# Units of four heads, spread MoE work and elementwise steps on GpSimd in a fused attention and MoE kernel

## The chip, the cores and the metric

The kernel runs on one core of a Trainium2 chip. Times are microseconds of device time of one launch; a kernel's time is the median of its runs. The profile describes one of these runs, taken with the hardware profiler; its "span" is the time from the first to the last instruction, and in the profiled run of the changed kernel the time is 1.8 us above the span. PE is the matrix engine, DVE the vector engine, ACT the scalar engine, POOL the GpSimd engine and SP the engine that only issues transfers here. "L230" is line 230 of the kernel in question; "MoE" is the program's name for the two dense products with an ELU between them.

## The reference

Eight batches of eight heads of 576 rows of 64 values go through an attention with exponential features. Their results, put side by side, are the 4608 rows of 512 values of the dense part.

```python
def phi(x):                                   # x: batch, head, 576, 64
    proj = np.einsum('bhsd,df->bhsf', x, w_phi)                    # 128 features
    proj = proj - np.max(np.abs(proj), axis=-1, keepdims=True)
    return np.concatenate([np.exp(proj), np.exp(-proj)], axis=-1)
q_p, k_p = phi(q), phi(k)
kv  = np.einsum('bhsf,bhsd->bhfd', k_p, v)
z   = np.sum(k_p, axis=2)
num = np.einsum('bhsf,bhfd->bhsd', q_p, kv)
den = np.einsum('bhsf,bhf->bhs', q_p, z)[..., None] + 1e-06
x   = (num / den)                             # as 4608 rows of 512
h   = x @ w_in                                # 512 -> 2048
g   = np.where(h > 0, h, np.exp(np.minimum(h, 0)) - 1)             # ELU
out = g @ w_out                               # 2048 -> 512
```

With m the largest |projection| of a row, the two halves of a row's features are exp(p) exp(-m) and exp(-p) exp(m). For a query row the factor exp(-m) falls out of num / den (but for the 1e-06), while the two halves keep different weights, 1 and exp(2m). The kernel before leaves that weight out. The changed kernel puts it back ("query maximum restored"), which is added work.

## The kernel before

One unit of attention is a pair of heads. Key maxima `m_k`, key exponentials `EK` and the factors `em` are made first; `em` scales the values into `vs`, on DVE, in many small pieces:

```python
for g0, gcnt in s_groups:                     # 3 groups of up to 2 row tiles
    ...                                       # pk: projection of the keys, in PSUM
    nc.vector.tensor_reduce(m_k[...], pk_v, axis=AX.X, op=ALU.max, apply_absolute_value=True)
    nc.scalar.activation(EK[..., 0, :], pk_v, ACT.Exp, scale=1.0)
    nc.scalar.activation(EK[..., 1, :], pk_v, ACT.Exp, scale=-1.0)
    nc.scalar.activation(em[:, 0, ...], m_k[...], ACT.Exp, scale=-1.0)
    nc.scalar.activation(em[:, 1, ...], m_k[...], ACT.Exp, scale=1.0)
    for hi in range(2):
        for sg in range(2):
            nc.vector.tensor_tensor(vs[hi][:, sg, ...], v_aug[hi][...], em[...], op=ALU.mult)
```

Then come the query exponentials `Eq`, the products `pkv` (keys by values) and `pn` (queries by `pkv`), and the division into `x_pair`, which five transposes turn for the dense part. The query maximum exists behind a switch that is off:

```python
EXACT_QMAX = False
...
if EXACT_QMAX:
    ...                                       # second projection, m_q, w_s = exp(2 m_q)
    nc.vector.tensor_tensor(tot, pnum[1], w_s[...], op=ALU.mult)
    nc.vector.tensor_tensor(tot, tot, pnum[0], op=ALU.add)
else:
    ...                                       # both halves summed in PSUM by PE
nc.vector.tensor_scalar_add(den, num_src[:, :, D], 1e-6)
nc.vector.reciprocal(rec, den)
nc.vector.tensor_tensor(x_pair[...], num_src[:, :, 0:D], rec..., op=ALU.mult)
```

In a unit of the first GEMM, the ELU takes three instructions: the exponential on ACT, and two on DVE.

```python
nc.scalar.activation(e_sb, ph, ACT.Exp)
nc.vector.tensor_scalar(u_sb, e_sb, 1.0, 1.0, op0=ALU.min, op1=ALU.subtract)
nc.vector.tensor_tensor(gT[:, jt], u_sb, ph, op=ALU.max)
```

All weights are loaded before the first q and k, on POOL's queue. A chunk of 512 rows becomes MoE work once its batches are done, and it is laid into the pairs by a quota of at least one GEMM unit per pair; what is left follows at the end.

The softmax here doesn't subtract the row's maximum and nothing guards it: scores larger than these inputs give would overflow.

## Time and profile before

| what | kernel before | where it is from |
|---|---|---|
| time | 530.67 us (527.86 to 531.39), 3 runs | timed runs |
| span, mean granted clock | 524.4 us, 0.948 | profiled run |
| busy: PE, DVE, ACT, POOL | 78%, 69%, 61%, 49% | totals of the page |
| first matmul | 26.9 us | order of time |
| two pairs of heads in the middle | 22.7 us (2 x 11.35; 27 pairs end by 334 us, the first at 39 us) | order of time |
| last two MoE chunks | 461 to 521 us | order of time |

A busy share is an average over the start, the middle and the end. Each has another limit here: transfers in the first 27 us, the serial chain of a pair up to 334 us, PE itself after that. The prediction below shows the lines in question.

### The profile page before, as it was taken

The page shows a single profiled execution, that of the slowest core. Times are in us where ns is not written, and L with a number is a line of the kernel's source. Part 1 is how long each engine was busy: PE and PEld are TensorE (multiplying, and loading weights), DVE is VectorE, ACT ScalarE, POOL GpSimd, SP SyncE. Part 2 cuts the span into 40 slices and gives each one's busy share as a digit, 9 for nine tenths or more (in the row PEclk, how much of TensorE's full clock was granted, in tenths as well). Part 3 has the DMA queues.
Part 4 walks back from the last instruction along what each step waited for, and adds up shares of the span by engine and source line. Part 5 has one row for each costly group of instructions (what it writes and reads, how often), then busy time and mean ns, then how long its engine had stood idle before and what let it go on. Part 6 is the DMA issues. An engine that isn't in the chain of part 4 may idle for free.

```text
span 524.4 us, 9742 instructions
## 1 busy us (share of the span) xinstructions
PE 408.5 (78%) x3200; PEld 222.5 (42%) x3200; DVE 364.1 (69%) x1358; ACT 319.5 (61%) x904; POOL 258.3 (49%) x400
## 2 busy tenths in 40 slices
PE   0056667678976679977789778977997999989997
PEld 0034444345543345534455444443544454434433
DVE  2055568989788988798986789479459579174470
ACT  0046568777568876787866788479257367153441
POOL 6299999967677767776676666460000000000000
PEclk9997668979989989998999899999999999989999
DMA  8989988955866756877567655660110100200102
GB/s 157 185 53 59 58 57 55 58 40 38 106 61 40 46 37 62 100 46 46 36 56 85 58 35 34 90 59 2 42 40 2 56 25 1 81 1 31 51 0 80
DMA packets 124817, 28.45 MB, mean 54 GB/s; under 512 B 117600, under 2 KB 119648, under 8 KB 124768
## 3 DMA queue, kind: packets, MB, share of 16 engines
q0 software_dynamic: 119584, 18.41, 47.7%
q1 hardware_dynamic: 5184, 9.44, 4.9%
q8 instruction: 25, 0.41, 0.3%
q14 instruction: 24, 0.20, 0.1%
HBM read 36.77 MB, written 9.44 MB: 88 GB/s over the span
## 4 chain that ended last, share of the span: by engine, by line
PE 49%; DVE 21%; ACT 21%; DMA 4%; issue 3%; POOL 1%; POOLq 0%; DVEq 0%; ACTq 0%
PE po L127 21%; PE ph L102 13%; DVE vs L243 5%; ACT EK L230 4%; ACT EK L227 4%; PE pk L212 4%; DVE gT L116 4%; DVE u_sb L112 4%; ACT Eq L266 4%; DVE x_pair L353 3%; DMA w_out_sb<-in_moe_w_out_dram 3%; PE pn L341 3%; PE tr L198 3%; ACT Eq L268 2%; PE xt L369 2%
## 5 line engine op out<-in xcount | busy, mean ns | idle before, releaser
L102 PE MATMUL ph<-xT_sb,w_in_sb 128*128 128x512 bf16 x576 | 158.9, 396 | 19.3 <-DVE gT L116 15.7
L127 PE MATMUL po<-w_out_sb,gT 128*128 128x512 bf16 x576 | 133.4, 379 | 0.3 <-DVE gT L116 0.2
L110 ACT ACTIVATE e_sb<-ph 128x512 f32<-128x512 f32 x144 | 85.2, 640 | 39.5 <-PE ph L102 39.1
L116 DVE TENSOR_TENSOR gT<-u_sb,ph 128x512 bf16<-128x512 bf16 x144 | 97.2, 681 | 1.8
L112 DVE TENSOR_SCALAR u_sb<-e_sb 128x512 bf16<-128x512 f32 x144 | 62.3, 442 | 42.4 <-ACT e_sb L110 41.8
L102 PEld LDWEIGHTS <-w_in_sb 128*128 128x128 bf16 x576 | 55.4, 101 | 75.8 <-issue 39.3
L243 DVE TENSOR_TENSOR vs<-v_aug,em 128x130 bf16<-128x130 bf16 (+1 forms) x384 | 75.6, 265 | 9.6 <-ACT em L233 9.1
L127 PEld LDWEIGHTS <-gT 128*128 128x128 bf16 x576 | 54.3, 98 | 59.6 <-issue 3.6
L168 POOL DMA_DIRECT2D q_pair<-in_q_dram x64 | 55.2, 866 | 43.4 <-PE tr L198 37.8
L266 ACT ACTIVATE Eq<-pq 128x288 bf16<-128x288 f32 x128 | 59.1, 462 | 24.6 <-PE pq L259 24.3
L220 DVE TENSOR_REDUCE m_k<-pk 128x4 f32<-128x512 f32 (+1 forms) x96 | 52.1, 594 | 14.3 <-PE pk L212 14.2
L268 ACT ACTIVATE Eq<-pq 128x288 bf16<-128x288 f32 x128 | 60.9, 476 | 0.0
L168 POOL DMA_DIRECT2D k_pair<-in_k_dram x64 | 57.1, 898 | 5.1 <-DMA w_out_sb<-in_moe_w_out_dram 4.4
L184 POOL DMA_DIRECT2D v_aug<-in_v_dram x64 | 53.7, 863 | 10.0 <-DVE den L351 5.2
L227 ACT ACTIVATE EK<-pk 128x512 bf16<-128x512 f32 (+1 forms) x96 | 52.5, 547 | 4.5 <-DVE m_k L220 4.5
L188 POOL DMA_DIRECT2D v_aug<-in_v_dram x64 | 40.8, 639 | 27.8 <-DVE vs L243 27.8
L276 PEld LDWEIGHTS <-EK 128*128 128x128 bf16 x640 | 32.4, 102 | 51.2 <-issue 20.1
L135 ACT COPY o_sb<-po 128x512 f32<-128x512 f32 x27 | 15.8, 586 | 62.0 <-PE po L127 62.0
L230 ACT ACTIVATE EK<-pk 128x512 bf16<-128x512 f32 (+1 forms) x96 | 53.5, 558 | 0.0
L259 PE MATMUL pq<-qTp,w_phi_both 128*128 128x288 bf16 x128 | 32.6, 300 | 19.9 <-ACT EK L230 18.6
L276 PE MATMUL pkv<-vs,EK 128*128 128x65 bf16 x640 | 36.1, 201 | 14.4 <-ACT EK L230 8.0
L174 POOL DMA_DIRECT2D k_pair<-in_k_dram x64 | 43.9, 685 | 4.5 <-DMA w_out_sb<-in_moe_w_out_dram 4.5
(46 smaller groups left out, 458.4 us busy)
## 6 DMA issues: line engine op xcount, KB each, us to landing
out_dram<-o_sb SPq DMA_DIRECT2D x36, 256.0 KB, 2.0
q_pair<-in_q_dram POOLq DMA_DIRECT2D x64, 64.0 KB, 2.6
k_pair<-in_k_dram POOLq DMA_DIRECT2D x64, 64.0 KB, 2.7
v_aug<-in_v_dram POOLq DMA_DIRECT2D x64, 64.0 KB, 2.8
w_in_sb<-in_moe_w_in_dram POOLq DMA_DIRECT2D x4, 512.0 KB, 7.1
w_out_sb<-in_moe_w_out_dram POOLq DMA_DIRECT2D x4, 512.0 KB, 15.9
q_pair<-in_q_dram POOLq DMA_DIRECT2D x64, 8.0 KB, 2.1
k_pair<-in_k_dram POOLq DMA_DIRECT2D x64, 8.0 KB, 2.3
```

The lines of the kernel that those rows point to most:

```text
L102: nc.tensor.matmul(ph[:, 0:csz], w_in_sb[:, ct, jt * P:(jt + 1) * P], xT_sb[:, ct, t0:t0 + csz], start=(ct == 0), stop=(ct == N_CT - 1),)
L110: nc.scalar.activation(e_sb[:, 0:csz], ph[:, 0:csz], ACT.Exp)
L112: nc.vector.tensor_scalar(u_sb[:, 0:csz], e_sb[:, 0:csz], 1.0, 1.0, op0=ALU.min, op1=ALU.subtract,)
L116: nc.vector.tensor_tensor(gT[:, jt, 0:csz], u_sb[:, 0:csz], ph[:, 0:csz], op=ALU.max)
L127: nc.tensor.matmul(po[0:tsz], gT[:, jt, tt * P:tt * P + tsz], w_out_sb[:, jt, :], start=(jt == 0), stop=(jt == N_JT - 1),)
L168: nc.gpsimd.dma_start(out=dst[:, 0:full_st, hi * D:(hi + 1) * D], in_=src[b, h, 0:full_st * P, :].rearrange("(t p) d -> p t d", p=P),)
L227: nc.scalar.activation(EK[:, g0:g0 + gcnt, :, 0, :], pk_v, ACT.Exp, scale=1.0)
L230: nc.scalar.activation(EK[:, g0:g0 + gcnt, :, 1, :], pk_v, ACT.Exp, scale=-1.0)
L243: nc.vector.tensor_tensor(vs[hi][:, sg, g0:g0 + gcnt], v_aug[hi][:, g0:g0 + gcnt], em[:, sg, g0:g0 + gcnt, hi:hi + 1].to_broadcast((P, gcn ...
L266: nc.scalar.activation(eq[:, 0, c0:c0 + half_S], pq, ACT.Exp, scale=1.0)
L268: nc.scalar.activation(eq[:, 1, c0:c0 + half_S], pq, ACT.Exp, scale=-1.0)
L276: nc.tensor.matmul(pkv[:, hi, sg, :], EK[:, ti, hi, sg, :], vs[hi][:, sg, ti, :], start=(ti == 0), stop=(ti == n_st - 1),)
```

## The change

The intent: fewer and larger instructions, DVE relieved, PE fed evenly. A unit of attention is four heads. The 64 tail rows of the heads are packed together. A chunk of 512 rows per batch is MoE work, spread over the two units of the next batch, step by step; the eight tails of 64 rows make the ninth chunk. q and k of the first unit are loaded ahead of the weights. The ELU's subtract, the scaling `vs` (and its tail `vst`) and the division `x` (and `xt`) go to POOL. The query maximum is back. The core of the diff:

```diff
 # 1. loads: q/k first, weights between the units' loads, v on SP's queue
-    for ct in range(N_CT):
-        nc.gpsimd.dma_start(out=w_in_sb[:, ct, :], in_=w_in_r[:, ct, :])
-    ...
+    load_quad(0)
+    load_tails(0, 4)
+    load_quad(1)
+    load_w_in()
+    load_quad(2)
+    load_w_out()
+    load_tails(4, NQ)
 # 2. vs: four heads' values, one instruction per head, on POOL
-                    nc.vector.tensor_tensor(
-                        vs[hi][:, sg, g0:g0 + gcnt],
-                        ...
+            for hh in range(4):
+                nc.gpsimd.tensor_tensor(
+                    vs[:, hh],
+                    vb[:, hh:hh + 1].to_broadcast((P, 2, NT, D1)),
+                    em[:, :, 4 * hh:4 * hh + 4, None].to_broadcast((P, 2, NT, D1)),
+                    op=ALU.mult,
+                )
+            ...                                   # vst: two more for the tails
 # 3. query maximum: a second projection per head, and a weighted sum on DVE
+        def q_head(hh):
+            project(st["qT"], hh, st["m_q"])
+            ...
+            nc.scalar.activation(w, st["m_q"], ACT.Exp, scale=2.0)
+            ...
+            nc.vector.tensor_tensor(tot, pn[1], st["w"][...], op=ALU.mult)
+            nc.vector.tensor_tensor(tot, tot, pn[0], op=ALU.add)
 # 4. division, on POOL
-            nc.vector.tensor_tensor(
-                x_pair[:, :, hi * D:(hi + 1) * D], ...
+                nc.gpsimd.tensor_tensor(
+                    st["x"][:, s, :, c, :],
+                    st["tot"][:, hh, :, 0:D],
+                    rec[:, 4 * hh:4 * hh + 4, None].to_broadcast((P, NT, D)),
+                    op=ALU.mult,
+                )
+            ...                                   # xt: one more for the tails
 # 5. ELU: subtract on POOL, minimum and maximum in one instruction on DVE
-        nc.vector.tensor_scalar(
-            u_sb[:, 0:csz], e_sb[:, 0:csz], 1.0, 1.0, op0=ALU.min, op1=ALU.subtract,
-        )
-        nc.vector.tensor_tensor(gT[:, jt, 0:csz], u_sb[:, 0:csz], ph[:, 0:csz], op=ALU.max)
+        nc.gpsimd.tensor_scalar(u_sb, e_sb, -1.0, 1.0, op0=ALU.add, op1=ALU.mult)
+        nc.vector.scalar_tensor_tensor(
+            gTs[ch][:, jt, :], u_sb, 0.0, ph, op0=ALU.min, op1=ALU.max
+        )
 # 6. MoE spread over the steps of the units
-                quota = max(1, len(pending_moe) // remaining_pairs)
+        share = len(pending) if qd == 1 else len(pending) // 2
+        for n, step in enumerate(steps):
+            step()
+            upto = share * (n + 1) // len(steps)
+            while done < upto:
+                pending.pop(0)()
+                done += 1
```

The steps of a unit are, in this order: transposes, five key projections, `k_scale` (makes em, vs, vst), five query projections, the query features, two `kv`, four heads of output, the tail, `divide`, and the transposes of x.

## The prediction

> **What bounds the kernel now.** I read the totals first, then the slices, then the start, then one head pair in order of time, then the end.
>
> ```profile
> span 524.4 us, 9742 instructions
> PE 408.5 (78%) x3200; PEld 222.5 (42%) x3200; DVE 364.1 (69%) x1358; ACT 319.5 (61%) x904; POOL 258.3 (49%) x400
> ...
> PE   0056667678976679977789778977997999989997
> ...
> DMA  8989988955866756877567655660110100200102
> ```
>
> No engine is full. PE is idle for 524.4 - 408.5 = 116 us: all of the first two slices (13.1 us each), some 30% of the long middle, little at the end. The order of time says why:
>
> ```profile
> 14.66 0.54 POOL L174 DMA_DIRECT2D q_pair<-in_q_dram  x1 [1.70 <-DMA w_in_sb<-in_moe_w_in_dram]
> ...
> 26.93 0.69 PE L198 MATMUL tr<-ident,q_pair 128*128 128x128 bf16 x5 [26.93 <-DMA q_pair<-in_q_dram]
> ```
>
> The q/k loads stand behind 4.2 MB of weights on one queue, and POOL, which issues them, itself waits until earlier loads land: the first matmul starts at 26.9 us. (That wait is the number to remember.) Then one pair of heads follows another on PE:
>
> ```profile
> 303.11 0.59 ACT L227 ACTIVATE EK<-pk 128x512 bf16<-128x512 f32 x1
> 303.59 0.60 ACT L230 ACTIVATE EK<-pk 128x512 bf16<-128x512 f32 x1
> 304.07 0.22 ACT L233 ACTIVATE em<-m_k 128x4 f32<-128x4 f32 x1
> ...
> 311.85 0.45 PE L369 MATMUL xt<-ident,x_pair 128*128 128x128 bf16 x5 [0.18 <-DVE x_pair L353]
> 312.14 0.44 PE L198 MATMUL tr<-ident,q_pair 128*128 128x128 bf16 x5
> ...
> 320.22 0.79 PE L341 MATMUL pn<-kv_sb,Eq 128*128 128x65 bf16 x20
> ...
> 323.32 0.45 PE L369 MATMUL xt<-ident,x_pair 128*128 128x128 bf16 x5 [0.18 <-DVE x_pair L353]
> ```
>
> The next pair's transposes come right after the last pair's xt, so pairs are a serial chain of PE, DVE and ACT steps: 323.32 - 311.85 = 11.5 us for this pair. From 27 to 334 us there are 28 such pairs, 10.9 us each, whatever MoE work is mixed in (some 15 of the 36 MoE matmuls that a pair's share would be). So two pairs, the unit that the change makes into one, take 22 us. MoE work is left over, and the last four pairs stretch to 20-29 us each, with PE nearly full. The last two chunks come after the last attention:
>
> ```profile
> 461.21 14.86 PE L102 MATMUL ph<-xT_sb,w_in_sb 128*128 128x512 bf16 x52 [1.44 <-DVE gT L116]
> 476.11 13.97 PE L127 MATMUL po<-w_out_sb,gT 128*128 128x512 bf16 x64
> 489.92 16.62 PE L102 MATMUL ph<-xT_sb,w_in_sb 128*128 128x512 bf16 x64
> 506.57 13.97 PE L127 MATMUL po<-w_out_sb,gT 128*128 128x512 bf16 x64
> ```
>
> 64 dense matmuls take 13.97 us (216 ns each); the first GEMM takes 16.62, since each of its 16 units needs DVE for u_sb and gT. The unit costs come from these groups:
>
> ```profile
> L116 DVE TENSOR_TENSOR gT<-u_sb,ph 128x512 bf16<-128x512 bf16 x144 | 97.2, 681 | 1.8
> L112 DVE TENSOR_SCALAR u_sb<-e_sb 128x512 bf16<-128x512 f32 x144 | 62.3, 442 | 42.4 <-ACT e_sb L110 41.8
> L220 DVE TENSOR_REDUCE m_k<-pk 128x4 f32<-128x512 f32 x64 | 41.4, 684 | 14.3 <-PE pk L212 14.2
> L353 DVE TENSOR_TENSOR x_pair<-pn,rec 128x320 bf16<-128x320 f32 x64 | 31.3, 489 | 0.1
> ```
>
> [...] The rows agree: 681 and 684 ns for 512. So the fused min/max on DVE should cost what gT costs now, and the query reduces what m_k costs. [...] here 64 KB land in 2.6 us.
>
> **The change part by part.**
>
> *Totals.* PE: MoE keeps 1152 matmuls of 512 columns. Attention goes from 222,000 to 249,000 columns (18 instead of 10 projections of 256 columns per four heads, fewer padded transposes); at 512 columns in 216 ns that is +11 us. DVE, as a sum of rows: out go u_sb 62, vs 78, memsets 29; in come query reduces 55 (as m_k) and the two tot operations (128 x 0.42 + tails 18 = 72, replacing x_pair 31); copies get larger and fewer. 408 becomes some 322 us. ACT: 424 becomes about 323, as 904 instructions become 580. POOL: 256 small loads shrink to some 60 loads (about 60 us of issue), and compute comes[...]. No engine is overfull: if throughput ruled, this would be some 450-480 us. But the chain rules.
>
> *The chain of one unit of four heads, without MoE.* In the compiled order the next unit's transposes still come after this unit's x transposes, and each unit is now: xT, kT and qT copies on DVE 2.5 us (two of 1024, at 0.66 scaled from the 512 and 640 copies, overlap PE); first reduce, 3.3; key exponentials on ACT, 8 x 0.48 + 2 x 0.27 = 4.4 (0.48 apart, as shown above) and em, 8.0; [...] The query exponentials lie beside that (ACT 8.4 to 13.0). kv matmuls and copies to 16.0; four tot multiplies and adds 8 x 0.4, tails 1.1, den and rec 0.5, with waits to 21.1; [...]transposes, 24.3. So 24.3 us against 22 for two pairs: the larger batch saves instructions, not latency, because POOL's two stages[...] and the query maximum sit on the chain.
>
> *MoE mixed in.* It is spread evenly now, 128 matmuls per batch (two units) in place of some 60 per four pairs. First unit of a batch, about 56 first-GEMM matmuls: four u_sb stand in POOL's queue behind vs/vst, and their gT stand in DVE's queue ahead of the first tot multiply (+1.5 us); further gT lie among the tot and den steps, and two u_sb ahead of x (+2.2). About 28 us. Second unit, 64 second-GEMM matmuls: 5 stand ahead of the first pn (+1.1), 16 between the second and third head (3.5 us of which 2.2 are not hidden), 16 between the last x transpose and the next unit's first transpose (+3.2). About 31 us. A batch: 59 us; seven batches: 413.
>
> *The start.* q/k go first, so PE starts near 6-10 us and the first key part is done by 20. But in POOL's order the first vs stands behind every load: two more units, all weights, all tails, each waiting for the load eight places before it. Scaled from the 21 us that the weights alone take: weights 21, six q/k loads 8, tails and v in 256-byte pieces 15-24. So the first vs starts near 45-50 us, the first unit ends at about 62, the second at 86, where the old kernel had four pairs done at 74. The gain of the early q/k is lost.
>
> *The end.* Four blocks of 64 matmuls at 13.9 with DVE off the first GEMM's path (0.68 against 1.1 us per unit[...]): 56 + 4 of drain = 60, against 66.
>
> Sum: 86 + 413 + 60 = 559 us of span, +6 as timed runs are above the span (530.7 against 524.4): 565. My waits are read pessimistically where several fall together (the old kernel hid 31 MoE matmuls in a pair for nothing), so I put the time at 552.
>
> **Rivals.** (1) Throughput rules: even spreading fills PE's holes, and a batch takes about 46-50 us: 470-500 us. For it: no engine above 70-80%, PE idle 30% in the middle, the last four pairs nearly PE-bound because of bad spreading. Against: units stay serial, and MoE sits at fixed places. (2) The start costs nothing: if POOL were free of load waits, batch 0 would end at 58, 28 us earlier: some 525-535, a draw. For it: loads of a unit are fewer and larger. Against: POOL's waits at 14.66.[...]
>
> **Range and chances.** Gain of the end -6, start +12, middle between -20 and +50. That gives 512 to 590. Faster by over 2% (under 520) 0.2: it needs rival 1. Within 2%: 0.2. Slower: 0.6.
>
> **What would show it.** Right: first tr before 12 us, but the first vs on POOL after 40 with DMA as what ended its wait; units 27-32 us apart by the x transposes, longer in the second of a batch; [...]POOL ahead of pkv and of the x transposes in the chain of waits; first GEMM at the end about 14 us. Wrong: batches under 52 us apart, [...]or POOL idle at 20-40 us without a DMA named.

The chain of a unit came to 24.3 us, a batch to 28 + 31 = 59 us, and the whole to 86 + 413 + 60 = 559 us of span, lowered to a time of 552. The +1.5 and +2.2 us in the first unit of a batch are estimates; their working isn't shown. Three other figures can be followed in the trace of the kernel before. The 0.42 us for a tot operation of 260 elements lie close to the line through 489 ns for 320 (x_pair) and 681 for 512 (gT), which gives 0.43. The 0.27 us of a tail exponential is the distance of two EK of 256 elements at 305.40 and 305.67 us. And "the load eight places before": seven issues from 9.74 to 26.16 us wait for a transfer there, three for w_in and four for w_out, and each time that is the tile which the load eight places before fills.

## More of the kernel before

For the comparison with the changed kernel, this is where the chain of work that ended last was spent. It is followed back from the last instruction, and each share is one of the span:

```profile
PE 49%; DVE 21%; ACT 21%; DMA 4%; issue 3%; POOL 1%; POOLq 0%; DVEq 0%; ACTq 0%
```

POOL is on it with 1%. It issues loads and does nothing else that anyone waits for in the middle.

## The result, and the profile after

The changed kernel takes 571.96 us (median of 4 runs, 570.74 to 574.21), beside 530.26 us (4 runs, 527.86 to 531.39) for the kernel before. The ratio is 1.0812, with a 95% interval of 1.077 to 1.0854: slower by 8%. A ratio here is the mean time of one kernel's runs over that of the other's of the same rounds, so it isn't quite the ratio of the medians quoted.

The page of the changed kernel, its totals, two rows of its 40 slices (busy tenths, 14.3 us a slice) and its chain of work that ended last:

```profile
span 572.4 us, 8389 instructions
PE 416.2 (73%) x3066; PEld 232.1 (41%) x3120; DVE 292.0 (51%) x647; ACT 264.8 (46%) x581; POOL 263.3 (46%) x392
...
PE   2302557768866786868787896778768867789996
POOL 7637234654365426551556236633644265426060
...
PE 31%; POOL 26%; issue 16%; DVE 11%; ACT 9%; DMA 6%; POOLq 0%; ACTq 0%; DVEq 0%
```

DVE has 72 us less to do than before and ACT 55 us less, and the kernel is slower all the same. PE is idle for 156 us instead of 116. The chain tells where the time went: POOL's share of it is 26% in place of 1%, DVE's and ACT's have fallen from 21% each to 11% and 9%. Work that was taken from DVE didn't leave the chain; it stands on it under another engine's name.

The granted clock (TensorE's, as a share of full speed) is no rival here. Its mean over the span is lower than before, 0.901 against 0.948, but over the attention part it is 0.93 (89 to 509 us) against 0.94 (27 to 458 us).

The groups of instructions that moved (busy time, mean ns of one, then the idle time of the engine before them and what ended it):

```profile
L448 POOL TENSOR_SCALAR u_sb<-e_sb 128x512 bf16<-128x512 f32 x144 | 88.1, 619 | 116.9 <-ACT e_sb L446 105.7
...
L230 POOL TENSOR_TENSOR vs<-v_main,em 128x520 bf16<-128x520 f32 x64 | 65.7, 1056 | 36.3 <-ACT em L224 36.3
L377 POOL TENSOR_TENSOR x<-tot,rec 128x256 bf16<-128x256 f32 x64 | 37.2, 614 | 92.1 <-DVE rec L374 91.0
```

The start, in order of time (start, duration, engine, line, operation, count; in brackets the engine's idle time before it and what ended it). First PE, then POOL:

```profile
7.09 1.03 PE L167 MATMUL tr<-ident,k_main 128*128 128x128 bf16 x8 [7.09 <-DMA k_main<-in_k_dram]
```

```profile
43.08 0.75 POOL L109 DMA_DIRECT2D q_tails<-in_q_dram  x1 [2.02 <-DMA w_out_sb<-in_moe_w_out_dram]
...
45.20 2.25 POOL L109 DMA_DIRECT2D v_tails<-in_v_dram  x3 [0.63 <-issue]
47.44 4.11 POOL L230 TENSOR_TENSOR vs<-v_main,em 128x520 bf16<-128x520 f32 x4
51.51 1.32 POOL L241 TENSOR_TENSOR vst<-v_tails,em 64x260 bf16<-64x260 bf16 x2
```

The first matmul is 20 us earlier than before. Yet POOL, which has the first `vs` to do, is held by loads until 47.44 us: from 22.6 us on nearly each of them waits for an earlier one to land, and `vs` stands behind all of them. The last of these loads are tails of units 4 to 15, which the first unit doesn't use. The first unit ends (last transpose of x) at 63.48 us.

A second unit of a batch in the middle, beside MoE work of the second GEMM (`po`):

```profile
309.57 0.42 ACT L224 ACTIVATE em<-m_k 128x18 f32<-128x18 f32 x2
...
310.07 4.10 POOL L230 TENSOR_TENSOR vs<-v_main,em 128x520 bf16<-128x520 f32 x4 [4.04 <-ACT em L224]
...
315.50 0.28 PE L289 MATMUL pkv<-vst,EKt 128*128 128x130 bf16 x2 [1.45 <-POOL vst L241]
...
318.06 0.66 PE L323 MATMUL pn<-kv,Eq 128*128 128x65 bf16 x16
...
318.55 3.62 PE L459 MATMUL po<-w_out_sb,gT 128*128 128x512 bf16 x15
...
322.00 0.65 PE L323 MATMUL pn<-kv,Eq 128*128 128x65 bf16 x16
...
325.71 2.33 POOL L377 TENSOR_TENSOR x<-tot,rec 128x256 bf16<-128x256 f32 x4 [9.56 <-DVE rec L374]
326.96 0.40 PE L394 MATMUL tr<-ident,x 128*128 128x128 bf16 x4 [0.61 <-POOL x L377]
```

From em to the first pkv 5.9 us pass, nearly all of them vs and vst on POOL; PE has done what MoE work stood ahead of pkv and waits for 1.45 us. The other 15 po that would have filled the wait stand two steps later, between the second and third heads' pn, and hold those up. From pn to the transposes of x there are 8.9 us, with x on POOL as their last link. The last transposes of successive units lie, from the second unit on, 31.7, 26.6, 32.8, 29.2, 32.5, 26.6 us apart, and so on: 60.05 us per batch on average, (509.06 - 88.73) / 7, where four pairs took 45.4 us before. More MoE work is done in this time than before, 128 matmuls per batch in place of some 73.

At the end, the two dense GEMMs now run at the same speed:

```profile
512.58 13.98 PE L438 MATMUL ph<-xT,w_in_sb 128*128 128x512 bf16 x63
```

That is 13.98 us where the kernel before needed 16.62. The subtract on POOL is only a part of this: in sub_dve and all_dve below, where it is on DVE again, the same block takes 14.84 us.

### The profile page after: what moved, and what is told of

The parts are those of the page before. It is cut to its first block, busy times and chain, and to the rows that moved or that the text cites. A ratio compares the mean times of both kernels' runs of the same rounds, so it can differ in the third digit from the quotient of the medians.

```text
span 572.4 us, 8389 instructions
## 1 busy us (share of the span) xinstructions
PE 416.2 (73%) x3066; PEld 232.1 (41%) x3120; DVE 292.0 (51%) x647; ACT 264.8 (46%) x581; POOL 263.3 (46%) x392
## 4 chain that ended last, share of the span: by engine, by line
PE 31%; POOL 26%; issue 16%; DVE 11%; ACT 9%; DMA 6%; POOLq 0%; ACTq 0%; DVEq 0%
POOL vs L230 11%; PE po L459 11%; PE ph L438 10%; POOL x L377 6%; ACT EK L216 6%; DVE gT L451 4%; POOL vst L241 3%; DMA w_out_sb<-in_moe_w_out_dram 3%; PE tr L167 3%; POOL u_sb L448 3%; DVE tot L332 2%; DVE tot L338 2%; PE pkv L300 2%; PE pk L196 2%; DMA w_in_sb<-in_moe_w_in_dram 2%
## 5 line engine op out<-in xcount | busy, mean ns | idle before, releaser
L438 PE MATMUL ph<-xT,w_in_sb 128*128 128x512 bf16 x482 | 136.1, 394 | 18.0 <-DVE gT L451 16.1
L448 POOL TENSOR_SCALAR u_sb<-e_sb 128x512 bf16<-128x512 f32 x144 | 88.1, 619 | 116.9 <-ACT e_sb L446 105.7
L451 DVE SCALAR_TENSOR_TENSOR gT<-u_sb,ph 128x512 bf16<-128x512 bf16 x144 | 95.7, 681 | 86.5 <-POOL u_sb L448 85.7
L230 POOL TENSOR_TENSOR vs<-v_main,em 128x520 bf16<-128x520 f32 x64 | 65.7, 1056 | 36.3 <-ACT em L224 36.3
L377 POOL TENSOR_TENSOR x<-tot,rec 128x256 bf16<-128x256 f32 x64 | 37.2, 614 | 92.1 <-DVE rec L374 91.0
L216 ACT ACTIVATE EK<-pk 128x512 bf16<-128x512 f32 x128 | 64.6, 633 | 24.3 <-DVE m_k L203 24.3
L259 ACT ACTIVATE Eq<-pq 128x512 bf16<-128x512 f32 x128 | 67.6, 712 | 4.7 <-PE pq L251 4.7
L289 PE MATMUL pkv<-vst,EKt 128*128 128x130 bf16 x64 | 11.2, 271 | 72.8 <-POOL vst L241 52.7
L203 DVE TENSOR_REDUCE m_q<-pk 128x4 f32<-128x512 f32 (+1 forms) x80 | 48.4, 634 | 10.0 <-PE pk L196 9.0
L196 PE MATMUL pk<-w_phi_both,qT 128*128 128x256 bf16 x144 | 28.1, 301 | 13.0 <-ACT EK L216 11.3
L196 PE MATMUL pk<-w_phi_both,kT 128*128 128x256 bf16 x144 | 25.0, 287 | 7.4 <-ACT EK L216 6.5
```

Of the source, the lines that this page charges most:

```text
L196: nc.tensor.matmul(pk[:, 2 * j:2 * j + 2, :].rearrange("p a b -> p (a b)"), xT[:, 2 * hh + j, :], w_phi_rhs, start=True, stop=True,)
L203: nc.vector.tensor_reduce(m[:, 4 * hh:4 * hh + 2 * n], pk[:, 0:2 * n, :], axis=AX.X, op=ALU.max, apply_absolute_value=True,)
L216: nc.scalar.activation(dst, pk, ACT.Exp, scale=1.0 - 2.0 * sg)
L230: nc.gpsimd.tensor_tensor(vs[:, hh], vb[:, hh:hh + 1].to_broadcast((P, 2, NT, D1)), em[:, :, 4 * hh:4 * hh + 4, None].to_broadcast((P, 2, ...
L259: nc.scalar.activation(st["Eq"][:, par, s, sg, :], pq, ACT.Exp, scale=1.0 - 2.0 * sg)
L377: nc.gpsimd.tensor_tensor(st["x"][:, s, :, c, :], st["tot"][:, hh, :, 0:D], rec[:, 4 * hh:4 * hh + 4, None].to_broadcast((P, NT, D)), op=A ...
```

## The experiments

Twelve kernels ran, in the groups in which they are told; all gave correct results to the test's tolerance. The medians of the kernel before were 527.8 to 528.7 us in these groups. Each expectation names its own theory and rival. The main theory was that POOL's new work lies on the chain of each unit and, at the start, behind the loads; the main rival that the larger units, the MoE work laid into them or the restored query maximum cost the time, whatever engine does what.

### vs and vst back on DVE (vs_dve)

```diff
-                nc.gpsimd.tensor_tensor(
+                nc.vector.tensor_tensor(
                     vs[:, hh],
 ...
-                nc.gpsimd.tensor_tensor(
+                nc.vector.tensor_tensor(
                     vst[r, :, :, s, :],
```

> vs and vst on DVE in every unit, the rest as changed. Theory (POOL's 5.4 us for vs and vst stand on each unit's chain, and hold back the u_sb behind them): 1.5 to 3 us less per unit, and unit 0's end moves from 63 to about 51 us as x still waits in POOL's queue: 515 to 540 us. Rival (the query exponentials on ACT end at the same time as vst, so the wait is only renamed): only the 12 us at the start, 555 to 562.

Measured: 515.87 us (514.53 to 516.57), ratio 0.9759 (0.9715 to 0.9803), 56 us less than the changed kernel, at the far edge of what the theory gave. The first unit ends at 53.88 us, 9.6 earlier, and a batch takes 53.7 us (30.95 and 22.76) instead of 60.05; seven batches make 44 us of it. A second unit of this kernel in order of time:

```profile
276.40 0.41 ACT L224 ACTIVATE em<-m_k 128x18 f32<-128x18 f32 x2
...
276.85 2.53 DVE L230 TENSOR_TENSOR vs<-v_main,em 128x520 bf16<-128x520 f32 x4
...
281.15 0.28 PE L289 MATMUL pkv<-vst,EKt 128*128 128x130 bf16 x2
...
282.64 0.81 PE L323 MATMUL pn<-kv,Eq 128*128 128x65 bf16 x16
...
289.22 0.40 PE L394 MATMUL tr<-ident,x 128*128 128x128 bf16 x4 [0.95 <-POOL x L377]
```

The stretch from em to pkv falls from 5.9 to 4.75 us, from pkv to pn from 2.56 to 1.49, from pn to the transposes of x from 8.9 to 6.6. Together that is 4.6 us, of which only the first stretch, 1.2 us, holds the scaling itself. The rest comes with it: the compiler has put most po ahead of pkv and single ones between the heads, so the block of 15 behind the second head is gone. This is a change of order that the edit brought about without naming it. How much of the 56 us belongs to DVE's speed and how much to the new order isn't separated by this run.

### x and xt back on DVE (x_dve)

```diff
-                nc.gpsimd.tensor_tensor(
+                nc.vector.tensor_tensor(
                     st["x"][:, s, :, c, :],
 ...                                    # and the same for st["xt"]
```

> x and xt on DVE in every unit, the rest as changed. Theory (POOL's 2.7 us of x stand alone on the chain[...]): 1.2 us less per unit, and up to 2 more where u_sb stand ahead of x: 535 to 553 us. Rival (hidden behind MoE matmuls that stand on PE ahead of the x transposes anyway): 565 to 572.

Measured: 556.5 us (556.09 to 557.25), ratio 1.0532 (1.0478 to 1.0586), 15.5 less than the changed kernel. The result lies outside both ranges, just above the theory's. Here one x took 508 ns and one xt 283, where POOL takes 614 and 396. Each unit is about 1 us shorter. x is on the chain, but a smaller part of it than vs.

### All four on DVE, in the first two units only (early_dve)

```diff
-                nc.gpsimd.tensor_tensor(
+                (nc.vector if i < 2 else nc.gpsimd).tensor_tensor(
                     vs[:, hh],
 ...                                    # and the same for vst, x and xt
```

> The changed kernel with vs, vst, x and xt of the first two units only on DVE; no load moves. Theory (POOL's own queue is blocked by the loads' waits until 47.4 us, and that alone holds unit 0): the first vs starts at about 20 us, unit 0 ends near 35 instead of 63 us, the whole is 28 to 32 us shorter, 540 to 545 us. Rival (the loads themselves are the limit, the wait moves to the weights or the tails at units 1 and 2): under 10 us shorter, above 562.

Measured: 537.3 us (536.04 to 538.93), ratio 1.0169 (1.0122 to 1.0217), 35 us less, a little more than was expected of the start. DVE and POOL in order of time:

```profile
20.59 2.52 DVE L230 TENSOR_TENSOR vs<-v_main,em 128x520 bf16<-128x520 f32 x4
...
28.58 0.76 POOL L109 DMA_DIRECT2D k_tails<-in_k_dram  x1 [1.89 <-DMA w_in_sb<-in_moe_w_in_dram]
```

The first vs starts at 20.59 instead of 47.44 us, while POOL goes on waiting for its loads. The first unit ends at 33.77 instead of 63.48 us. So most of 30 us of the changed kernel (26.9 us of them the later vs) are POOL standing behind loads. That vs_dve gained only 9.6 us in its first unit fits this: it leaves x on POOL, behind the same loads.

### Smaller blocks of the second GEMM (po_quarters)

```diff
-    def mm2(ch, tt):
+    def mm2(ch, tt, part):             # po is kept from part 0 to part 3
-        for jt in range(N_JT):
+        for jt in range(4 * part, 4 * part + 4):
 ...
-            lambda tt=tt: mm2(ch, tt) for tt in range(CHUNK // P)
+            lambda tt=tt, part=part: mm2(ch, tt, part)
+            for tt in range(CHUNK // P) for part in range(4)
```

> The second GEMM's units of 16 matmuls are emitted as four units of 4, so that MoE work is spread evenly by matmuls over the steps. Theory (the blocks of 16 matmuls at fixed places on PE cost 5 to 6.5 us of each batch): 535 to 555 us. Rival (blocks cost nothing, the chain is the bound and blocks fill its waits): 566 to 578.

Measured: 569.14 us (568.83 to 569.46), ratio 1.077 (1.0725 to 1.0816), 2.8 less by the medians. Its interval overlaps that of the changed kernel, so a gain isn't shown. The second unit of a batch got shorter (25.41 instead of 26.96 us), the first longer (34.38 instead of 33.09): the work moved from one to the other. The rival held. The blocks are gone from the two places named in the prediction, between the second and third heads and after the transposes of x, and the batch is as long as before. But one of 17 po now stands at the end of each first unit, and in the unit from 269 to 304 us PE waits for 4.15 us with the first GEMM, whose u_sb stand behind vs and vst on POOL. So blocks at these two places are not what makes a batch long; a kernel without any block wasn't run.

### Without the query maximum (no_qmax)

```diff
-            + [each(q_head, hh) for hh in range(5)]
 ...
-            nc.scalar.activation(w, st["m_q"], ACT.Exp, scale=2.0)
+            nc.vector.memset(w, 1.0)
```

> The changed kernel without the query projections for the maximum, their reduces and the exponential of w (w is set to 1: same result form as the kernel before); tot's multiply and add stay. Theory (DVE's query reduces lie beside ACT's exponentials and POOL's vs, off the chain): 0 to 0.7 us per unit, 560 to 572 us. Rival (the restored maximum is what made the change slow): over 1.5 us per unit, under 548 us.

Measured: 558.38 us (555.84 to 559.07), ratio 1.0556 (1.0509 to 1.0603), 13.6 less: 0.85 us per unit. This is nearer to the theory than to the rival, just below the range of the one. The multiply and the add of `tot` stay in this kernel, so the run undoes the projections, the reduces and one small exponential alone.

### The kernel before with its query maximum on (before_exact)

```diff
-EXACT_QMAX = False
+EXACT_QMAX = True
```

> The kernel before with its own switch for the exact query maximum on: per pair three more projections and reduces (1.6 us of DVE), two tot multiplies and adds of 325 elements (about 1.9 us of DVE, on the chain). Theory (pairs are serial, so DVE work added after kv lengthens each): 2 to 3 us for each of some 28 pairs, 575 to 610 us, so the change is no loss like for like. Rival (hidden beside MoE work): 530 to 550 us, and the change loses even like for like.

Measured: 609.32 us (608.59 to 610.83), ratio 1.1532 (1.1486 to 1.1579). The theory held, at the upper end of its range. The 1.6 us of its reduces fit the key reduces of the kernel before (52.1 us over 32 pairs), and the 1.9 us of its tot operations fit four times the 489 ns of an x_pair of 320 elements. In the old structure the same restoration costs 81 us (0.1532 of 528.7): DVE goes from 364 to 457 us of busy time. So the two kernels don't do the same work. Like for like, the changed kernel takes 1.0812 / 1.1532 = 0.938 of the time.

### Two units interleaved (pipelined)

The second half of unit i (kv to the transposes of x) is emitted among the first-half steps of unit i + 1.

```diff
-        return ([transposes] + ... + [q_features_tail] + [each(kv, c) ...] + ...)
+        front = [transposes] + ... + [q_features_tail]
+        back = [each(kv, c) for c in range(2)] + ... + [out_tail, divide, x_out]
+        return front, back
 ...
-        steps = attention_steps(i)
+        steps = merged(units[i][1], nxt) if nxt else list(units[i][1])   # nxt: front of i + 1
```

> The changed kernel with the second half of a unit (kv to x_out) emitted among the steps of the next unit's first half (transposes to query features), engines as changed. Theory (units are slow because they are a serial chain, with every engine half idle): a batch falls from 60 to 46 to 52 us, 480 to 520 us, the start still at 47 us. Rival (the 4 PSUM buffers of attention[...] hold it as before): above 550 us.

Measured: 542.11 us (541.64 to 543.04), ratio 1.0261 (1.0213 to 1.0309), 30 less. That is between the theory and the rival: the serial chain does cost time, but half-units beside each other did not bring the throughput back. Order of time shows what took the place of the old wait:

```profile
271.17 4.10 POOL L230 TENSOR_TENSOR vs<-v_main,em 128x520 bf16<-128x520 f32 x4
...
276.63 2.37 POOL L451 TENSOR_SCALAR u_sb<-e_sb 128x512 bf16<-128x512 f32 x4
...
278.02 2.29 PE L441 MATMUL ph<-xT,w_in_sb 128*128 128x512 bf16 x5 [4.38 <-DVE gT L454]
```

Four u_sb stand in POOL's queue behind vs and vst (5.4 us together); until they are done no gT can be made, and PE waits for 4.38 us with the first GEMM. POOL now holds up the MoE work rather than the attention. Nor is all of the gain in the middle: over the six batches from the second unit to the fourteenth, a batch takes 57.0 us against 59.8, 17 us in all. Another 17 us come from the last batch, because the last unit has no next first half beside it (12.9 instead of 26.6 us).

### vs, vst, x and xt back on DVE, the subtract still on POOL (vs_x_dve)

The edits of vs_dve and x_dve together.

> vs, vst, x and xt on DVE in every unit; only the ELU subtract stays on POOL. Theory (both POOL stages stand on the chain, savings add: 56 + 15 us, and unit 0 no longer waits for POOL at all, 12 more): 485 to 503 us. Rival (DVE, at 68% with vs alone, becomes the bound): 510 to 520 us.

Measured: 487.98 us (486.57 to 489.76), ratio 0.9235 (0.9189 to 0.928): 84 less than the changed kernel and 40 less than the kernel before. The theory held. The first unit ends at 33.56 us, a batch takes 52.7. Alone, the two edits gave 56 and 15.5; together they also free the start, which gives most of the 28 us beyond vs_dve (the first unit ends 20 us earlier). As in vs_dve, the block of po between the second and third heads' pn is gone. The chain of work that ended last:

```profile
DVE 36%; PE 33%; ACT 17%; issue 9%; DMA 2%; POOL 2%; POOLq 0%; DVEq 0%; ACTq 0%
```

POOL is down from 26% to 2%. DVE is on the chain with 36%, and it is busy for 78% of the span, with PE at 84%.

### Interleaved, with vs and x on DVE (pipe_vsx)

The edits of pipelined and vs_x_dve together.

> Both repairs at once: vs, vst, x and xt on DVE, and the second half of a unit among the next unit's first half. Theory (with POOL's queue out of the way, the overlap of units shows, as no u_sb stands behind vs any more): a batch near 46 to 48 us against 52.7 with vs and x on DVE alone, 450 to 470 us. Rival (DVE, 78% busy with vs and x on it, is now the bound): 478 to 490 us.

Measured: 495.98 us (494.34 to 497.79), ratio 0.9404 (0.9365 to 0.9444), slower than vs_x_dve without the interleaving. The theory fell, and the rival's range was missed as well. The seven batches take 51.89 us each on average, but that counts the last unit, which is short (12.2 us, with no next first half beside it). Over the six batches before it a batch takes 53.4 us against 53.0 in vs_x_dve: with POOL off the chain, this interleaving gained nothing in the middle. The first unit ends at 45.0 us, 11 later, as its second half is laid among the next unit's first; the short last unit gives most of that back. What is left of the 8 us is in the middle (3 us) and at the end, where 31 po stand after the last unit in place of 12:

```profile
429.30 7.07 PE L462 MATMUL po<-w_out_sb,gT 128*128 128x512 bf16 x31
```

### The same, with smaller blocks of the second GEMM (pipe_quart_vsx)

The edit of po_quarters added to pipe_vsx.

> As pipe_vsx, with the second GEMM's units in quarters as in po_quarters. Theory (overlapped units leave no hole for a block of 16 to fill, so finer blocks help): 3 to 12 us below pipe_vsx. Rival (as in po_quarters, work only moves to the other unit of the batch): within 5 us of pipe_vsx.

Measured: 480.11 us (479.28 to 482.0), ratio 0.9108 (0.9078 to 0.9138): 16 less than pipe_vsx, in the expected direction and more than was expected. Smaller blocks gained at most 2.8 us in the changed kernel and 16 here: 12.6 in the six batches (51.3 us each in place of 53.4), and 5 at the end, where 8 po are left over in place of 31. This is the fastest kernel, 9% below the kernel before, with the query maximum in it. In the middle (65 to 417 us) PE is busy for 309.6 of 352 us.

### Only the subtract back on DVE (sub_dve)

```diff
-        nc.gpsimd.tensor_scalar(
+        nc.vector.tensor_scalar(
             u_sb, e_sb, -1.0, 1.0, op0=ALU.add, op1=ALU.mult
```

> The changed kernel with only the ELU subtract back on DVE (0.44 us each); vs and x stay on POOL. Theory (much of POOL's cost is that u_sb queue behind vs/vst and so hold gT, PE and the buffers): the first unit of a batch falls by 2 to 3 us, less 0.4 us for each subtract on DVE's part of the chain, 550 to 568 us, with the last first-GEMM block back at about 16.5 us. Rival (DVE's added 62 us simply lengthens the units): 585 to 610 us.

Measured: 596.69 us (595.69 to 598.19), ratio 1.1315 (1.1282 to 1.1349), 25 more than the changed kernel. The rival held: this part of the move to POOL is a gain, though POOL takes 619 ns for it and DVE 554 in this kernel. The theory's side claim, a last first-GEMM block of 16.5 us, failed too: it takes 14.84.

### vs, x and the subtract on DVE (all_dve)

The edits of vs_x_dve and sub_dve together: no arithmetic of a unit is left on POOL.

> vs, vst, x, xt and the subtract all on DVE, units serial: what the move of the subtract to POOL is worth by itself, against vs_x_dve. Theory (with nothing else on POOL the subtract there is nearly free, and DVE is 78% busy without it): 500 to 525 us, 12 to 37 us above vs_x_dve. Rival (the extra hop between engines costs as much as it saves): 480 to 495 us.

Measured: 550.34 us (549.82 to 551.67), ratio 1.0437 (1.0402 to 1.0473), above the theory's range. It came from another group of runs than vs_x_dve, so the two are compared by their ratios: 1.0437 - 0.9235 = 0.120 of some 528 us, 63 us. The subtract on DVE, and DVE's wait for pn (us in total, times, longest):

```profile
L448 DVE TENSOR_SCALAR u_sb<-e_sb 128x512 bf16<-128x512 f32 x144 | 58.1, 419 | 28.0 <-ACT e_sb L446 27.5
...
DVE tot L332 <- PE pn L323: 50.5, 23, 3.5
```

The subtract is 58 us of work, but DVE is busy for only 31 us more than in vs_x_dve (412.9 against 381.6 us), in part because vs and x are faster here. The other half of the difference is idle time: DVE waits 50.5 us for pn, where vs_x_dve has 18.6. That wait goes with another change of order that the edit brought about without naming it. The block of po between the second and third heads' pn is back, as in the changed kernel:

```profile
292.66 3.62 PE L459 MATMUL po<-w_out_sb,gT 128*128 128x512 bf16 x16
```

What DVE's work costs and what this order costs isn't separated.

With this run, four kernels make a square (ratios to the kernel before):

| | subtract on POOL | subtract on DVE |
|---|---|---|
| vs, vst, x, xt on POOL | 1.0812 (changed) | 1.1315 (sub_dve) |
| vs, vst, x, xt on DVE | 0.9235 (vs_x_dve) | 1.0437 (all_dve) |

The two moves aren't independent. Taking vs and x off POOL gains 83 us beside a subtract on POOL, and 46 beside one on DVE (0.0878 of 528 us). The start gives 33 us in both columns: the second unit ends at 56 us in place of 89. The seven batches give 51 us in the left column and 12 in the right. In the right column the block of po stands in both kernels; in the left one it goes with the move.

### What the parts are worth

Put in one order, the runs divide the change into four steps, each a difference of two ratios times 528 us:

| step | from, to | worth |
|---|---|---|
| query maximum restored, in the old structure | before, before_exact | +81 us |
| units of four, packed tails, q/k first, MoE spread, min/max fused | before_exact, all_dve | -58 us |
| subtract to POOL | all_dve, vs_x_dve | -63 us |
| vs, vst, x and xt to POOL | vs_x_dve, after | +83 us |

The sum is +43 us, the 8% of the result. Each step is good to some 3 us, by the intervals of the ratios. The sizes depend on the order in which the steps are taken. In the changed kernel the query maximum is worth 14 us (without tot's multiply and add) and the subtract 25, and the last step is 46 us if the subtract is on DVE. The last two steps also include what the compiler's order changed.

## Why the prediction was right or wrong

The direction was right, the time was 20 us short, and the range held it. By its steps:

| step of the prediction | predicted | measured |
|---|---|---|
| first matmul | 6 to 10 us | 7.09 |
| first vs, behind the loads | 45 to 50 | 47.44 |
| first unit ends | 62 | 63.48 |
| second unit ends (batch 0) | 86 | 88.73 |
| a batch in the middle | 59 | 60.05 (60.5 as booked in the prediction) |
| end | 60 | 63.3 (59.9 as booked) |
| first GEMM at the end | 13.9 | 13.98 |
| vs, vst, x, xt on POOL | | 1.056, 0.619, 0.614, 0.396 us |
| u_sb on POOL | | 0.619 us |
| sum, as a span | 559 us | 572.4 |

The end is measured from the last transpose of x, at 509.06 us. A block of 16 po of 3.4 us follows there first, which the prediction booked in the second unit before it. Without it the end is 59.9 us, and the seven batches are (420.3 + 3.4) / 7 = 60.5 us each. The same block explains why the trace has first units of 33.1 us and second ones of 27.0, where the prediction had 28 and 31: six of the seven first units hold a block. Moved back, they are about 30.2 and 30.4, so the first was 2.2 us longer than predicted and the second 0.6 shorter. The prediction's test, "longer in the second of a batch" by the x transposes, fails as it was written.

**The step that failed is the last one, "so I put the time at 552".** The terms summed to 559 us of span and were within 2.4% of it. The prediction then took 13 us off for waits read pessimistically. The trace shows no such slack: the terms were 1.5 us short per batch (10.7 in all) and 2.7 in batch 0, 13.4 together. The "+6" from span to time wasn't there either: within one run the two differ by 1.8 us. The profile of the kernel before, with a span of 524.4 us, had simply been one of a faster execution than the median. With neither the shading nor the 6, the sum would have been 559 + 2 = 561.

**POOL on the chain: right.** vs_x_dve, which differs only in the engine of vs, vst, x and xt, takes 84 us off, more than the whole loss. The page's 26% of the chain was the sign. The durations of POOL's instructions that the prediction used, the trace it had doesn't show; the table above has what was measured in the changed kernel. The prediction added them to a fixed order. In the runs the order changed with the engine: the middle gains 51 us where the block of po goes, and 12 where it stays and DVE has the subtract. That the move costs 83 us is shown; that POOL's durations alone make the batch long isn't.

**POOL behind the loads at the start: right.** In early_dve the second unit ends at 57 us in place of 88.7; the second rival named 58. That rival's own claim, that the start costs nothing, is refuted by the same run.

**Query maximum on the chain: right in kind, small in size.** Counted among the causes of a longer chain, it is worth 0.85 us per unit. That leaves out the multiply and add of tot, which no run took from this kernel.

**The blocks of po: the booking was right, the mechanism was not.** The prediction charged 1.1 + 2.2 + 3.2 us per batch to three blocks that can't be hidden. Taken from the two costliest of these places, they give back at most 0.4 us per batch (2.8 over 7), which is within the noise. The grain mattered only after POOL was off the chain and two units overlapped; quarters without the overlap weren't run.

**What it overlooked.** It took the moves to POOL as one thing. They are two with opposite signs: the subtract belongs to MoE work that has slack in the middle, and there it frees DVE (25 to 63 us, by where vs and x are); vs and x belong to the chain, and there the move costs (46 to 83 us, by where the subtract is). The first rival's 470 to 500 us, which the prediction gave to even spreading, are real (vs_x_dve 488, pipe_quart_vsx 480), but only with vs and x off POOL.

**Readings of the kernel before that were off.** By 334 us 27 pairs have ended, not 28. They lie 11.35 us apart, so two take 22.7 us, and the last five stretch (17 to 30 us), not four. Four pairs held some 73 MoE matmuls, not 60, and POOL issued 384 small loads, not 256. The three parts of the range give 516 to 586 us, not 512 to 590. None of this enters the sum of 559.

**What stays open.** In vs_dve, vs_x_dve and all_dve the compiler's order changed along with the engine, and the share of each wasn't separated. Nor did a run move the loads themselves, which would test the start from the other side.

## What to carry to other kernels

Ask of each instruction moved to a slower engine (one vs took 1056 ns on POOL and 790 on DVE in vs_dve) whether it belongs to the chain that sets the end or to work that fills its gaps: here the move to POOL lost 46 to 83 us for work of the first kind (vs and x) and gained 25 to 63 us for work of the second (the subtract). Read the compiled order again after each edit; in three runs here (vs_dve, vs_x_dve, all_dve) it changed along with the engine. Before giving compute to an engine that also issues loads, read what stands ahead of it in that queue; here the first multiply waited until 47 us for loads that it didn't need. And when the terms of a sum are each read from the profile, don't shade the sum by feeling.

## What single instructions and loads took

- vs, x, vst and xt on POOL, in the changed kernel: with one input broadcast, 520 elements took 1056 ns and 256 took 614. A line through the two has 1.67 ns per element and some 0.19 us fixed; it gives 620 and 399 ns for 260 and 128 elements, where vst took 619 and xt 396. On DVE one vs took 695 ns in all_dve and 790 in vs_dve, so POOL took 1.5 and 1.3 times as long.
- The subtract, with one input: 619 ns on POOL, 419 (all_dve) to 554 (sub_dve) on DVE. It took longer on POOL, and yet the kernel gained 25 us (beside vs and x on POOL) to 63 us (beside them on DVE) by having it there.
- The same instruction took different times in different kernels. u_sb on POOL took 619 ns with vs on POOL, 656 in vs_dve, 675 in vs_x_dve and 694 in pipe_quart_vsx. On DVE, vs took 695 ns in all_dve, where POOL has no arithmetic of a unit, but 790 in vs_dve and 827 in pipe_quart_vsx, where it has; x took 419 ns in all_dve and 462 in vs_x_dve, while tot (from PSUM and SBUF) took 424 in both. What causes this isn't shown.
- What held POOL until 47.44 us: in the changed kernel ten load issues from 22.62 to 43.08 us wait for a transfer, four for w_in, one each for k_main and q_main, four for w_out, and each time that is the tile which the load eight places before fills (at 22.62 us the first w_in). So 40 loads stood ahead of the first vs, which needed none of the last of them.
